# A fused state-space and SwiGLU kernel on one core: the hand-written order of steps rewritten behind step 150, outputs of a pair in two steps, weight powers in two passes, last bank in two halves

## The chip, the core and the metric

One core of a Trainium2 chip. The metric is the time of the kernel on the device in microseconds (us); the kernel before was run three times for its median, and one more execution was recorded by the profiler. TensorE (PE) does the matrix products, VectorE (DVE), ScalarE (ACT) and GpSimd (POOL) the rest, SyncE (SP) issues the transfers.

## The reference

Batch 4, 8 heads, 768 steps, head size 32, 16 states; the result of the first part is read as 3072 tokens of 256 numbers for the second.

```python
for c in range(nc):                       # chunks of 32 steps
    cum = np.cumsum(la, axis=-1)          # la = log a
    L = np.exp(cum[..., :, None] - cum[..., None, :]) * causal
    M = np.einsum('bhin,bhjn->bhij', Cc, Bc) * L
    y_intra = np.einsum('bhij,bhjd->bhid', M, xc)
    y_inter = np.einsum('bhin,bhnd->bhid', Cc, state) * np.exp(cum)[..., None]
    y[:, :, sl] = y_intra + y_inter
    state = decay_full * state + sum_j(B_j x_j decay_from_j)
x = y.transpose(0, 2, 1, 3).reshape(3072, 256)
xn = x / np.sqrt(np.mean(x * x, axis=-1) + 1e-6) * rms_g
out = (silu(xn @ w_gate) * (xn @ w_val)) @ w_out      # 256 -> 1536 -> 256
```

## The kernel before, in words

**Tiles.** The 3072 tokens are 12 *pairs* p of 256 tokens (the state-space part works on them, in halves of 64 tokens from pair 2 on) and 6 *blocks* of 512 tokens (two pairs each; the feed-forward part works on them). The 1536 hidden features are 12 tiles f of 128.

**The state-space part of a pair**, by steps: `x` loads the values (SyncE), `qb`/`qc` load the squares of B and C, `vB`/`vC` turn them, `Tt` and `Td` make the transposed factors T, `spread`, `sub`, `ex`, `ca` make the decays L of a group of heads, `A` multiplies x by the decayed B (TensorE, 28 small products of 32x64), `S` adds that into the running state (VectorE, needs `A`), `y` makes the pair's outputs: first 12 or 16 products of T with the states (recorded as y<-T,S), then 32 products of L with x (y<-L,x). The recorded counts are twice these, since a 4-byte product runs as two passes. The outputs of the two pairs of a block share four banks of PSUM.

**The feed-forward part of a block**, by steps: `sq`, `sqa`, `ms`, `rs`, `rb`, `xn` make the norm. Block 0's features 0 and 1 are multiplied with the outputs before the norm (`early`), which is put on behind. `xH`, `xL`, `xK` split the normed values into three parts, and `X.blk.f.m` (m: 0 gate, 1 value) multiplies them as six products of 128x512. In block 0, features 2 to 7 are multiplied whole instead (`F.blk.f.m`, four passes). Behind `X` or `F` stand `silu` (ScalarE) and `hid` (VectorE, gate times value), then `hH`, `hL`, `hK` split the hidden features, and `OX.blk.f.b` multiplies them with the weights of the way out into bank b of the block's two (block 0: whole, `OF`). Blocks 1 to 4 make their output transposed with 128x512 products (L1197), the last block in 128x256 products (L1203), two groups of 128 tokens in a bank. `put.blk.b` copies a bank of results and issues the transfers out: in blocks 1 to 4 a transpose on VectorE and four transfers, in blocks 0 and 5 a copy (`put` on ScalarE, `putv` on VectorE) and two transfers.

**The weights.** `fetch` loads a strip of weights, `pow` (L272, ScalarE) makes from the high 16 bits of each word the power of two of its exponent, in three passes, `man` (L301) and `wt` (L307) use it on VectorE to form the weight, `wH`, `wL`, `wM` its three parts.

**What sets the order.** No scheduler: one string, `order`, lists 1177 steps, each named with its group (`i:` first steps and weights, `p:` pairs, `b:` blocks), its kind and its numbers. They are emitted in this order, and every engine executes its own instructions in the order in which they were emitted. Buffers come from rings (8 banks of PSUM, and on the on-chip memory 22 and later 29 places of 128x512 and four smaller rings). A place goes back to its ring when its counted uses are through, so the order also decides which buffer an instruction writes to and whom it waits for.

Of the kernel before, what the change touches and what calls it, by code (L numbers as in the profile page):

```python
# [9 lines left out]
FP32 = mybir.dt.float32  # L10
F32R = mybir.dt.float32r
# [39 lines left out]
def kernel(  # L51
# [222 lines left out]
    def power(k):  # L274
        words16, u, shape = fetched[k]
        n = shape[1] * shape[2]
        parts[k, "eb"] = eb = h.take(1, "e")
        e = eb.tile
        g = e.rearrange("p (a b) -> p a b", a=shape[1])
        b16 = e.bitcast(I16)[:, 0:n].rearrange("p (a b) -> p a b", a=shape[1])  # L280
        activation(out=g, in_=words16, func=AF.Relu, scale=1.0 / 16, bias=kinks[:, 0:1])
        activation(out=g, in_=g, func=AF.Prelu, scale=-1.0, bias=kinks[:, 1:2],
                   alpha=2.0 ** -20)
        activation(out=b16, in_=g, func=AF.Prelu, scale=-2.0 ** 27, bias=kinks[:, 2:3],
                   alpha=2.0 ** -20)
        parts[k, "e"] = b16
# [3 lines left out]
    def uses_whole(k):  # L290

        if k < 2:
            return 2
        f = 2 * (k // 2) if k < 12 else 2 * (k - 12)
        return sum((gv_mode(blk, g) == 4) if k < 12 else 2 * ((blk, g) in O4)
                   for g in (f, f + 1) for blk in range(NBLK))
# [70 lines left out]
    kinks = const.tile([P, 3], FP32, name="kinks")  # L367
# [501 lines left out]
    yts, sqs = {}, {}  # L869
# [37 lines left out]
    def outputs(p):  # L907

        n, blk = p % 2, p // 2
        if n == 0:  # L910
            ps["y", blk] = [bank((P, 512), 2, "y") for u in range(4)], set()
        (four, opened), s = ps["y", blk], st[p]

        def product_y(k, u, i, rows, **operands):
            o = four[2 * k + u][1]
            nc.tensor.matmul(out=o[rows, (2 * n + i) * HC:(2 * n + i + 1) * HC],  # L916
                             start=(k, u, rows.start) not in opened, stop=True,
                             skip_group_check=True, **operands)
            opened.add((k, u, rows.start))

        for i in range(2):
            for q in range(NQ):
                for u in range(2):
                    if (2 * p) % NC == 0 and i == 0 and u == 0:
# [3 lines left out]
                    product_y(q // 2, u, i, slice(o, o + 64),  # L928
                              lhsT=S[r].rearrange("p t d -> p (t d)"),
# [3 lines left out]
        opened |= {(k, u, o) for k, u, o_ in opened for o in (o_, o_ + 32)}  # L933
        for i in range(2):
            for hd in range(NH):
                for u in range(2):
                    o = 32 * ((hd + 2 * u) % 4)
                    product_y(hd // 4, u, i, slice(o, o + 32), lhsT=s["x"][halves[u], i, hd],
                              rhs=Ls[p][halves[u], i, hd], tile_position=(HC * u, o))
        s["xb"].used()  # L940
        s["Tb"].used()
# [118 lines left out]
    def modes(blk):  # L1060
        return [gv_mode(blk, f) for f in range(NF)]

    def x_high(blk, t, scaled):
        n = modes(blk).count(3)
        xparts[blk, t, 0] = b = h.take(2 * n + 2, "xh")
# [3 lines left out]
    def x_part(blk, t, i):  # L1069

        xparts[blk, t, i] = b = h.take(2 * modes(blk).count(3), "x" + "hlk"[i])
# [13 lines left out]
    GV4 = {(0, 2), (0, 3), (0, 4), (0, 5), (0, 6), (0, 7)}  # L1085
    O4 = {(0, 0), (0, 1), (0, 2), (0, 3), (0, 4), (0, 5), (0, 6), (0, 7), (0, 8), (0, 9), (0, 10), (0, 11)}

    def gv_mode(blk, f):
        return 0 if blk == 0 and f < 2 else 4 if (blk, f) in GV4 else 3

    def uses_of_x(blk):
        return 6 * (3 in modes(blk)) + 2 * modes(blk).count(4)
# [19 lines left out]
    def normed(f):  # L1112
        banks, gv = ps.pop(("gv", f))
        us[0, f] = h.take(2, "u")
        hx[0, f] = h.take(2, "hx")
# [12 lines left out]
    def hidden(f):  # L1128
        v = view(hx[0, f], [P, TB])
        ub = us.pop((0, f))  # L1130
        nc.vector.tensor_tensor(out=v, in0=view(ub, [P, TB]), in1=v, op=ALU.mult)
# [23 lines left out]
    def silu_gv(blk, f):  # L1155
# [3 lines left out]
                   scale=GAIN if blk == 0 and gv_mode(0, f) == 3 else 1.0)  # L1159
        b.used()  # L1160

    def hide_gv(blk, f):
        v = view(hx[blk, f], [P, TB])
        b, o = gvs.pop((blk, f, 1))
        if (blk, f) in O4 and (blk or gv_mode(blk, f) == 4):
            nc.vector.tensor_tensor(out=v, in0=v, in1=o, op=ALU.mult)
        else:
            nc.vector.scalar_tensor_tensor(out=v, in0=o, scalar=GAIN, in1=v, op0=ALU.mult,  # L1168
                                           op1=ALU.mult)
        b.used()  # L1170

    def hid_high(blk, f, scaled):
        hh[blk, f] = b = h.take(4, "hh")
# [3 lines left out]
    def hid_part(blk, f, i, engine=nc.vector):  # L1177

        (hl, hk)[i - 1][blk, f] = b = h.take(2, "h" + "hlk"[i])
# [9 lines left out]
    OT = {1, 2, 3, 4}  # L1189

# [94 lines left out]
    def token_out():  # L1285
# [46 lines left out]
        "A": additions, "S": states, "y": outputs,  # L1332
# [16 lines left out]
        "OF": o_whole, "OX": o_split,  # L1349
        "put": lambda blk, b: put(blk, b, ac.copy),  # L1350
# [32 lines left out]
        i:wM.10 i:wL.10 b:exps.4 i:wL.6 b:X.0.11.0 p:vB.5 i:fetch.16 b:X.0.8.0 b:hid.0.2 i:wt.14
        b:rb.1 p:spread.11 i:man.15 i:wt.11 i:wM.2 p:dT.4 i:wHv.11 p:spread.10 i:wt.15 i:wH.7
        i:pow.13 p:scale.5 b:OF.0.5.0 p:subp.11 b:OF.0.4.0 i:man.9 b:hid.0.7 p:qc.4 p:vB.4 i:pow.9
        p:vC.5 i:fetch.17 b:X.0.10.0 i:wM.11 i:wH.4 b:OF.0.6.0 i:wt.13 i:wL.11 p:x.5 p:qb.6 b:xn.1.1
        b:OF.0.7.1 b:xn.1.0 i:wt.9 b:silu.0.9 b:OF.0.4.1 b:OF.0.1.1 b:xH.1.1 b:OF.0.7.0 p:sub.8
        b:X.0.11.1 b:xH.1.0 i:wH.9 b:OF.0.6.1 i:wM.3 b:X.0.10.1 b:OF.0.5.1 i:wL.9 b:silu.0.8 i:wM.9
        b:X.0.8.1 b:silu.0.10 b:xK.1.0 b:xL.1.0 p:qb.7 b:silu.0.11 p:ex.11 b:hid.0.11 p:x.4
        b:X.0.9.1 i:pow.16 p:ca.11 b:hid.0.8 p:ex.8 b:xK.1.1 b:xL.1.1 i:wH.12 b:OF.0.2.0 i:man.16  # L1390
        p:vC.4 b:hid.0.3 b:X.1.10.0 b:hid.0.9 i:wH.13 p:Tt.4.1 b:hid.0.10 p:ca.8 p:vB.7 i:pow.17
        b:X.1.1.0 i:man.17 i:wL.7 p:spread.9 b:X.1.11.1 i:wL.3 b:OF.0.3.0 b:X.1.11.0 p:scale.4
        b:silu.1.10 b:silu.1.1 i:wt.17 p:x.6 p:A.4 i:wM.0 i:wt.16 p:S.4 p:Tt.5.1 b:X.1.10.1
        b:OF.0.8.1 p:qb.9 p:A.5 p:sub.9 p:Tt.5.0 p:qc.6 p:subp.10 p:ex.10 b:OF.0.11.0 p:vB.6
        b:hid.1.10 p:ex.9 p:ca.9 b:OF.0.8.0 b:OF.0.10.0 p:ca.10 b:OF.0.9.0 p:dT.5 p:S.5 p:Tt.4.0
        i:wH.17 b:silu.1.11 b:gb.2 i:wL.4 b:X.1.0.0 i:wH.5 i:wL.5 i:wM.7 b:OF.0.2.1 b:L.2.3 i:wL.13
        b:OF.0.11.1 b:L.2.0 b:L.2.1 b:OF.0.10.1 b:silu.1.0 b:hid.1.11 p:Td.4 i:wH.14 b:L.2.2 p:vC.6
        p:qc.9 p:Td.5 p:scale.6 b:X.1.9.0 p:qc.7 b:hH.1.10 p:y.4 b:put.0.0 p:y.5 b:X.1.0.1 p:vB.9
        b:sq.2.0 p:x.7 i:wH.15 b:silu.1.9 b:X.1.1.1 p:spread.12 b:sq.2.1 i:wM.5 b:OF.0.3.1 p:vC.7
        b:yt.2.0 p:scale.9 i:wM.12 b:X.1.6.0 i:wM.4 p:A.6 b:yt.2.1 b:hK.1.10 p:dT.6 b:silu.1.6  # L1400
        b:sqav.2 b:X.1.5.1 i:wM.17 i:wH.16 p:spread.13 p:subp.12 b:hid.1.1 i:wL.17 b:X.1.5.0 b:ms.2
        p:spread.14 b:OF.0.9.1 p:ex.12 p:S.6 b:X.1.9.1 b:table.4 i:wM.13 b:put.0.1 b:silu.1.5
        p:scale.7 i:wL.16 p:Tt.7.1 b:rs.2 i:wM.16 i:wL.12 b:hH.1.1 b:X.1.2.0 i:exps b:hid.1.0
        b:X.1.3.0 p:spread.15 b:rb.2 p:vC.9 p:Tt.6.1 p:qb.10 b:hH.1.11 b:hid.1.9 b:hid.1.5 b:hH.1.0
        b:X.1.4.1 p:A.7 p:sub.14 b:silu.1.2 b:X.1.8.1 p:sub.13 b:hK.1.0 p:qb.8 p:S.7 b:X.1.8.0
        p:Tt.7.0 b:silu.1.8 b:X.1.4.0 b:hLp.1.1 p:ex.14 b:hid.1.8 b:hL.1.10 p:sub.15 b:X.1.6.1
# [113 lines left out]
```

## Time and profile before

| | |
|---|---|
| median of 3 runs | 369.09 us (368.76 to 369.15) |
| the profiled execution | 368.75 us, of which the span from first to last instruction is 367.0 us |
| mean granted TensorE clock | 0.998 |
| busy: TensorE, VectorE, ScalarE, GpSimd | 360.1, 276.7, 203.1, 75.0 us |
| recorded instructions: TensorE, VectorE, ScalarE | 3293, 514, 346 |
| feature products, three-part, L1150 | 768 in three groups of 83.0, 79.4 and 79.1 us |
| moved by transfers | 27.95 MB |

Busy times are sums over the whole span. Products are pipelined, so a recorded length (400 ns for a 128x512 product) is longer than the distance between the starts of two of them; where it matters, starts are compared. In the chain of waits, "issue" is time in which an engine waited for nothing that the profile shows, "SPq" is SyncE's queue at work on an instruction.

### The profile page before, as it was taken

Reading aid. Unit: us, or ns where it says so; the run is one execution under the profiler, and the core shown is the slowest. Engines: PE = TensorE matmul, PEld = TensorE weight load, DVE = VectorE, ACT = ScalarE, POOL = GpSimd, SP = SyncE. Lnnn points to the kernel's source line nnn. Section 1 sums busy time; section 2 is a strip of 40 time slices with the busy share of each in tenths; the row PEclk is TensorE's granted clock in tenths of the full one; section 3 lists DMA queues with packets and bytes.
Section 4 is the critical chain, followed back from the end, with each engine's and each line's share of the span. In section 5 each row is a group of like instructions: output and inputs, shape, how many; then the busy total and the mean of one; then the engine's idle time right before and its main releaser. Section 6 shows DMA issues by size and latency. Waiting matters only on the chain.

```text
span 367.0 us, 8226 instructions
## 1 busy us (share of the span) xinstructions
PE 360.1 (98%) x3293; PEld 280.8 (77%) x3293; DVE 276.7 (75%) x514; ACT 203.1 (55%) x346; POOL 75.0 (20%) x79
## 2 busy tenths in 40 slices
PE   8999989999999999999999999999999999999995
PEld 5677455887887777787877778877888888888895
DVE  6899897998998699875867896656447595346790
ACT  3899959999658864486237577034630222421310
POOL 4032010022301311352102316100303001131350
PEclk9999999999999999999999999999999999999999
DMA  7979872564564323542114210110000002001011
GB/s 104 207 136 275 220 292 43 170 143 105 91 120 104 107 47 78 121 63 63 33 30 121 63 29 2 30 30 2 7 29 2 0 10 50 0 0 29 2 30 57
DMA packets 94702, 27.95 MB, mean 76 GB/s; under 512 B 77544, under 2 KB 92616, under 8 KB 94664
## 3 DMA queue, kind: packets, MB, share of 16 engines
q1 hardware_dynamic: 92584, 27.30, 32.6%
q8 instruction: 26, 0.43, 0.5%
q10 hardware_dynamic: 2080, 0.13, 0.4%
q14 instruction: 12, 0.10, 0.1%
HBM read 23.68 MB, written 3.74 MB: 75 GB/s over the span
## 4 chain that ended last, share of the span: by engine, by line
PE 87%; SPq 3%; DVE 3%; ACT 2%; DMA 2%; issue 2%; POOL 0%; ACTq 0%; POOLq 0%; DVEq 0%
PE gv L1150 44%; PE o L1197 18%; PE o L1203 7%; PE gv L1140 4%; PE y L916 3%; PE gv L1105 2%; SPq L186 2%; PE g L766 2%; PE A L831 1%; DMA bq<-in_B_dram 1%; PE g L759 1%; DMA wr<-in_moe_w_out_dram 1%; ACT e L272 1%; SPq L654 1%; PE y L892 1%
## 5 line engine op out<-in xcount | busy, mean ns | idle before, releaser
L272 ACT ACTIVATE hx<-gv 128x512 f32<-128x512 f32 x70 | 40.4, 597 | 90.4 <-PE gv L1150 46.5
L1150 PE MATMUL gv<-xh,wh 128*128 128x512 f32 x256 | 83.0, 405 | 0.0
L1150 PE MATMUL gv<-xl,wp 128*128 128x512 f32 x256 | 79.4, 391 | 0.0
L1150 PE MATMUL gv<-xk,wp 128*128 128x512 f32 x256 | 79.1, 390 | 0.0
L1078 POOL TENSOR_TENSOR hl<-hx,hh 128x512 fp32r<-128x512 f32 x27 | 40.2, 1499 | 150.4 <-PE o L1197 99.5
L1168 DVE SCALAR_TENSOR_TENSOR hx<-gv,hx 128x512 f32<-128x512 f32 x64 | 43.0, 683 | 27.1 <-PE gv L1150 20.6
L1080 DVE SCALAR_TENSOR_TENSOR hk<-hx,hh 128x512 fp32r<-128x512 f32 x60 | 47.5, 810 | 18.6 <-PE o L1197 14.4
L1150 PEld LDWEIGHTS gv<-xl,wp 128*128 128x128 f32 x256 | 48.0, 188 | 10.8 <-DVE xl L1078 0.4
L1150 PEld LDWEIGHTS gv<-xk,wp 128*128 128x128 f32 x256 | 48.0, 188 | 10.4 <-DVE xk L1080 0.2
L1150 PEld LDWEIGHTS gv<-xh,wh 128*128 128x128 f32 x256 | 46.6, 188 | 11.0 <-issue 1.1
L1197 PE MATMUL o<-hh,wh 128*128 128x512 f32 x96 | 37.9, 395 | 0.0
L1197 PE MATMUL o<-hl,wp 128*128 128x512 f32 x96 | 37.4, 389 | 0.0
L1197 PE MATMUL o<-hk,wp 128*128 128x512 f32 x96 | 37.3, 389 | 0.0
L329 ACT ACTIVATE hh<-hx 128x512 fp32r<-128x512 f32 x35 | 21.6, 626 | 25.3 <-PE o L1197 15.8
L1078 DVE TENSOR_TENSOR hl<-hx,hh 128x512 fp32r<-128x512 f32 x33 | 24.1, 729 | 9.9 <-PE o L1197 7.6
L272 ACT ACTIVATE e<-e,kinks 128x512 f32<-128x512 f32 (+1 forms) x36 | 26.0, 722 | 1.2
L323 DVE SCALAR_TENSOR_TENSOR wp<-wh,w 128x512 fp32r<-128x512 f32 x36 | 24.6, 702 | 0.6 <-ACT wh L329 0.5
L632 POOL TENSOR_SCALAR_AFFINE_SELECT L<-L 64x512 f32<-64x512 f32 (+1 forms) x22 | 17.1, 776 | 34.1 <-ACT L L272 32.3
L1203 PE MATMUL o<-w,hx 128*128 128x256 f32 x96 | 23.5, 385 | 0.0
L1140 PE MATMUL gv<-xn,w 128*128 128x512 f32 x48 | 22.4, 603 | 0.0
L266 ACT ACT_TABLE_LOAD x17 | 21.8, 1283 | 1.1 <-PEq L1504 0.8
L1197 PEld LDWEIGHTS o<-hh,wh 128*128 128x128 f32 x96 | 18.0, 188 | 4.1 <-issue 0.2
(173 smaller groups left out, 525.4 us busy)
## 6 DMA issues: line engine op xcount, KB each, us to landing
L<-rowd SPq DMA_DIRECT2D x32, 128.0 KB
x<-in_x_dram SPq DMA_DIRECT2D x24, 128.0 KB
wr<-in_moe_w_out_dram SPq DMA_DIRECT2D x6, 511.5 KB
wr<-in_moe_w_gate_dram SPq DMA_DIRECT2D x5, 511.5 KB
wr<-in_moe_w_val_dram SPq DMA_DIRECT2D x5, 511.5 KB
out_dram<-ob SPq DMA_DIRECT2D x32, 64.0 KB
bc<-in_B_dram SPq DMA_DIRECT2D x23, 64.0 KB
bc<-in_C_dram SPq DMA_DIRECT2D x23, 64.0 KB
```

Source lines behind the costliest of these rows:

```text
L266: nc.scalar.preload_act_table_set("natural_log_exp_and_others")
L272: nc.scalar.activation(**operands)
L323: nc.vector.scalar_tensor_tensor(out=(low_parts, mixed_parts)[i][k], in0=high_parts[k], scalar=(-UP, GAIN)[i], in1=view(ws[k], shape), op0 ...
L329: nc.scalar.activation(out=out, in_=in_, func=AF.Copy, scale=scale)
L632: nc.gpsimd.affine_select(out=L[r], in_=L[r], pattern=[[0, L.shape[1]], [1, HC]], compare_op=ALU.is_ge, fill=0.0, base=0, channel_multipli ...
L1078: engine.tensor_tensor(out=out, in0=v, in1=high, op=ALU.subtract)
L1080: nc.vector.scalar_tensor_tensor(out=out, in0=v, scalar=REST, in1=high, op0=ALU.mult, op1=ALU.subtract)
L1140: nc.tensor.matmul(out=o, lhsT=view(ws[k], fetched[k][2])[:, t, f % 2 * P:][:, 0:P], rhs=xn[:, t], start=(t == 0), stop=(t == 1))
L1150: nc.tensor.matmul(out=o, lhsT=weights_of(m, t, f)[part], rhs=view(x, [P, TB], F32R), start=(part == t == 0), stop=(part == 2 and t == 1))
L1168: nc.vector.scalar_tensor_tensor(out=v, in0=o, scalar=GAIN, in1=v, op0=ALU.mult, op1=ALU.mult)
L1197: nc.tensor.matmul(out=o, lhsT=w[:, b * P:(b + 1) * P], rhs=v, start=opens, stop=True, skip_group_check=True)
L1203: nc.tensor.matmul(out=o[:, j * DM:(j + 1) * DM], lhsT=v[:, tk], rhs=w, start=opens, stop=True, skip_group_check=True)
```

## The change

The first 150 steps of `order` stay as they are. All steps behind them stand in another order, and there are 1200 steps in all. Four pieces of code change with it:

- `y` becomes two steps, `yi` (the products with the states) and `ya` (those with x), so that other steps can stand between them.
- `power` makes its result in two passes on ScalarE. The constants in `kinks` are two.
- For the second bank of the last block, the 12 steps `OX.5.f.1` (six products each) and `put.5.1` (a 128x512 copy on ScalarE, two transfers) are replaced by 24 steps `OY.f.j` (three products each), which fill one bank for each 128 tokens j, and by `puta.1` (ScalarE) and `putva.0` (VectorE), each a copy of 128x256 and one transfer.
- Whether a feature of block 0 uses whole weights can be chosen for gate and value apart; the set that is chosen is the same as before. `hide_gv` always uses the form of the product that also scales.

```diff
-        activation(out=g, in_=words16, func=AF.Relu, scale=1.0 / 16, bias=kinks[:, 0:1])
-        activation(out=g, in_=g, func=AF.Prelu, scale=-1.0, bias=kinks[:, 1:2],
+        activation(out=g, in_=words16, func=AF.Prelu, scale=-1.0 / 16, bias=kinks[:, 0:1],
                    alpha=2.0 ** -20)
-        activation(out=b16, in_=g, func=AF.Prelu, scale=-2.0 ** 27, bias=kinks[:, 2:3],
+        activation(out=b16, in_=g, func=AF.Prelu, scale=-2.0 ** 27, bias=kinks[:, 1:2],
                    alpha=2.0 ** -20)
...
-        for k, v in enumerate((1152.0, 256.0, -1792.0 * 128.0)):
+        for k, v in enumerate((-896.0, -1792.0 * 128.0)):
...
-    def outputs(p):
...
+    def outputs_of_states(p):
+        s = st[p]
         for i in range(2):
             for q in range(NQ):
                 for u in range(2):
...
+                    product_y(p, q // 2, u, i, o, 64, lhsT=S[r].rearrange("p t d -> p (t d)"),
                               rhs=s["T"][r, i, 3, halves[u]], tile_position=(32 * q, o))
...
+    def outputs_of_chunks(p):
+        s, blk = st[p], p // 2
         for i in range(2):
             for hd in range(NH):
                 for u in range(2):
...
+                    product_y(p, hd // 4, u, i, o, 32, lhsT=s["x"][halves[u], i, hd],
                               rhs=Ls[p][halves[u], i, hd], tile_position=(HC * u, o))
...
+    def product_apart(f, j):
+        if j not in apart:
+            apart[j] = bank((P, DM), NF + 1, "o")
+        place, o = apart[j]
+        tk = slice((2 + j) * P, (3 + j) * P)
+        for k, w in enumerate(out_weights_of(f)):
+            v = (hh, hl, hk)[k][NBLK - 1, f]
+            nc.tensor.matmul(out=o, lhsT=view(v, [P, TB], F32R)[:, tk], rhs=w,
+                             start=place.uses == NF + 1 and k == 0, stop=True,
+                             skip_group_check=True)
+            v.used()
+        place.used()
+
+    def put_apart(j, copy):
+        ob = h.take(1, "ob")
+        out_sb = view(ob, [P, DM])
+        place, o = apart[j]
+        copy(out=out_sb, in_=o)
+        rows = slice(T - (2 - j) * P, T - (1 - j) * P)
+        nc.sync.dma_start(out=out[rows], in_=out_sb)
...
-        b:OX.5.0.0 b:putv.5.0 b:OX.5.2.1 b:OX.5.1.1 b:put.5.1
+        b:OY.4.1 b:OY.2.1 b:OY.1.1 b:putv.5.0 b:OY.1.0 b:puta.1 b:putva.0
```

**TensorE around pairs 2 and 3.** Before, in program order (gv are feature products, here whole ones of block 0; A the additions of pair 2 and then 3; the rows with y the outputs of pair 2 and then 3; counts are instructions in the program):

```order
L1140 MATMUL gv<-xn,w 128x512 x8
L831 MATMUL A<-x,Bd 32x64 x12
L1140 MATMUL gv<-xn,w 128x512 x2
L831 MATMUL A<-x,Bd 32x64 x16
L1140 MATMUL gv<-xn,w 128x512 x2
L916 MATMUL y<-T,S 64x64 x16
L916 MATMUL y<-L,x 32x64 x32
L1140 MATMUL gv<-xn,w 128x512 x2
L916 MATMUL y<-T,S 64x64 x12
L916 MATMUL y<-L,x 32x64 x32
```

Now, on the same engine at the same place:

```order
L1149 MATMUL gv<-xn,w 128x512 x6
L830 MATMUL A<-x,Bd 32x64 x28
L1149 MATMUL gv<-xn,w 128x512 x6
L916 MATMUL y<-T,S 64x64 x16
L916 MATMUL y<-L,x 32x64 x32
L916 MATMUL y<-T,S 64x64 x12
L916 MATMUL y<-L,x 32x64 x32
L1149 MATMUL gv<-xn,w 128x512 x4
```

The additions of the two pairs now stand side by side, three feature steps stand between them and the outputs (one before), and the outputs of the two pairs stand side by side.

**SyncE around the values of pair 5.** Before (bc<-in_C with bc<-in_B in the row above it is a `qc` step, bq<-in_B a `qb` step; the first x row is pair 5, the second pair 4, the third pair 6):

```order
L173 DMA bc<-in_B_dram 128x8x16 x2
L186 DMA bc<-in_C_dram 128x1x128 x2
L238 DMA wr<-in_moe_w_out_dram 128x2x1023
L205 DMA x<-in_x_dram 128x8x32 x2
L186 DMA bq<-in_B_dram 128x1x128 x4
L205 DMA x<-in_x_dram 128x8x32 x2
L654 DMA L<-rowd 64x512 x2
L205 DMA x<-in_x_dram 128x8x32 x2
```

Now (the first x row is pair 4, the second pair 6, the third pair 5; the two qc steps are those of pairs 6 and 7):

```order
L205 DMA x<-in_x_dram 128x8x32 x2
L653 DMA L<-rowd 64x512 x2
L173 DMA bc<-in_B_dram 128x8x16 x2
L186 DMA bc<-in_C_dram 128x1x128 x2
L205 DMA x<-in_x_dram 128x8x32 x2
L173 DMA bc<-in_B_dram 128x8x16 x2
L186 DMA bc<-in_C_dram 128x1x128 x2
L205 DMA x<-in_x_dram 128x8x32 x2
```

The values of pair 5 were the first of the three to be issued and are now the last, behind the squares of pairs 6 and 7.

**SyncE at the end of the program.** Before, the transfers out of block 4 (32x16x32) and of block 5:

```order
L1229 DMA out_dram<-ob 32x16x32 x16
L1236 DMA out_dram<-ob 128x256 x4
```

Now:

```order
L1260 DMA out_dram<-ob 32x16x32 x16
L1267 DMA out_dram<-ob 128x256 x2
L1218 DMA out_dram<-ob 128x256 x2
```

The last four transfers are the same in number and size; the last two now belong to two copies.

More of the change, by code (lines that the diff above doesn't have):

```diff
@@ L905, in first_outputs, with outputs_of, product_y @@
         s["Tb"].used()
-    def outputs(p):
[L909 to L919, printed above, removed]
+    def outputs_of(p):
+        if p // 2 not in yparts:
+            yparts[p // 2] = [bank((P, 512), 2, "y") for u in range(4)], set()
+            ps["y", p // 2] = yparts[p // 2]
+        return yparts[p // 2]
+    def product_y(p, k, u, i, first, n, **operands):
+        four, opened = outputs_of(p)
+        groups = {(k, u, r) for r in range(first, first + n, 32)}
+        o = four[2 * k + u][1]
+        nc.tensor.matmul(out=o[first:first + n, (p % 2 * 2 + i) * HC:(p % 2 * 2 + i + 1) * HC],
+                         start=not groups & opened, stop=True, skip_group_check=True, **operands)
+        opened |= groups
+    def outputs_of_states(p):
+        s = st[p]
         for i in range(2):
```

277 lines of the change are left out of this document (140 added, 137 removed).

## The prediction

> **What bounds the kernel now.** I read the page's busy times first, then the chain of waits, then who waited for whom, then single stretches.
>
> ```profile
> PE 360.1 (98%) x3293; PEld 280.8 (77%) x3293; DVE 276.7 (75%) x514; ACT 203.1 (55%) x346; POOL 75.0 (20%) x79
> PE 87%; SPq 3%; DVE 3%; ACT 2%; DMA 2%; issue 2%; POOL 0%; ACTq 0%; POOLq 0%; DVEq 0%
> PE y L916 <- issue: 1.3, 2, 1.0
> ```
>
> TensorE is busy for 360.1 of 367.0 us, it is 87% of the chain, and the list of its waits (third line) has nothing above 1.3 us. The change keeps every product: the last block's second bank gets the same 128x256 products in another arrangement, and the set of features with whole weights is the same. So TensorE's work cannot shrink by arithmetic. What can shrink is the time around it: waits, the passage from big to small products and back, and the tail. What can grow is waiting for the other engines. A busy TensorE hides short gaps, so I read its starts:
>
> ```profile
> 138.03 0.39 PE L1197 MATMUL o<-hl,wp 128*128 128x512 f32 x1
> 138.26 0.39 PE L1197 MATMUL o<-hk,wp 128*128 128x512 f32 x1
> 138.58 0.46 PE L916 MATMUL y<-T,S 32*64 32x64 f32 x24
> 138.97 0.86 PE L916 MATMUL y<-L,x 64*32 64x64 f32 x64
> 139.76 0.50 PE L1197 MATMUL o<-hh,wh 128*128 128x512 f32 x1
> 140.09 0.40 PE L1197 MATMUL o<-hl,wp 128*128 128x512 f32 x1
> 140.33 0.39 PE L1197 MATMUL o<-hk,wp 128*128 128x512 f32 x1
> 141.06 0.31 PE L916 MATMUL y<-L,x 64*32 64x64 f32 x6
> 141.72 0.80 PE L916 MATMUL y<-L,x 64*32 64x64 f32 x58 [0.35 <-issue]
> ```
>
> Starts of a big product are 0.23 us apart (138.03, 138.26). The step into the small ones takes 0.32 us (138.26 to 138.58), the first big one behind them 0.33 us (139.76 to 140.09).
>
> **Term A: fewer passages between big and small products.** Going in costs 0.32 - 0.23 = 0.09 us, the first big one 0.10 us. The group of 64 ends at 138.97 + 0.86 = 139.83; a small product is recorded as 0.22 us long (row below), so its last one started at 139.61, and 0.15 us pass until 139.76. One island of small products thus costs 0.09 + 0.15 + 0.10 = 0.34 us beside its work. Two kinds of small product side by side cost one such 0.15 us: the 24 end at 139.04, the last of them started at 138.81, the next kind starts at 138.97.
>
> ```profile
> L916 PE MATMUL y<-L,x 64*32 64x64 f32 x640 | 9.1, 224 | 1.3 <-issue 1.3
> ```
>
> From the first step behind the products of the raw y (early) to the end, the steps of before make 29 islands with 11 joints inside them (10 of them the two halves of a pair's outputs); those of after make 20 islands with 20 joints, since A.2 stands beside A.3, y of pair 2 beside pair 3, A.5 beside A.4, A.7 beside A.6 and ms.2. That is 9 x 0.34 - 9 x 0.15 = 1.7 us less. Three of the pairs' outputs are now split by big products (pairs 6, 8, 10); they are counted in the 20. If joints cost nothing the term is 3.1 us, if they cost as much as an island it is nearly 0; the rows above say 0.15, so I take -1.7. [...]
>
> **Term B: two waits inside small products.**
>
> ```profile
> 44.69 0.39 PE A L831 x32
> 45.08 1.91 PE gv L1140 x4
> 46.99 1.10 PE y L916 x78
> 48.09 0.99 issue
> 49.09 0.33 PE y L916 x11
> ...
> 138.65 1.18 PE y L916 x76
> 139.83 0.89 PE o L1197 x3
> 140.72 0.66 PE y L916 x38
> 141.37 0.35 issue
> 141.72 0.80 PE y L916 x51
> ```
>
> In y.2 TensorE stands until 49.09, though its last product started at 48.09 - 0.22 = 47.87: 1.2 us. In y.7 it stands from 141.06 + 0.31 - 0.22 = 141.15 to 141.72: 0.57 us. The profile names no releaser ("issue"). I read them as the instruction stream running dry:
>
> ```profile
> q8 instruction: 26, 0.43, 0.5%
> ```
>
> 26 packets of 0.43 MB are 16.5 KB each, and 2 x 3293 products and weight loads over 26 are 253 instructions a packet, so a block of 256. I counted blocks through TensorE's order (a 4-byte product is two passes, so four instructions). The block before the first wait starts in A.3 (44.69) and the next falls at the end of y.2; the block before the second starts in y.6 (138.65) and ends in the middle of y.7. Resumption comes 49.09 - 44.69 = 4.4 us and 141.72 - 138.65 = 3.1 us after those starts: the next block needs that long, and the dense stretches ran through theirs in 3.2 and 2.5 us. In the new order the first of these blocks holds the rest of A.3, three whole products of 1.72 us each (1.91 less the island's ends) and y.2: about 6.5 us, over 4.4. The second holds three products of block 1's outputs (0.68 us each) where there was one: 2.5 + 1.36 less the part of y that left it gives about 3.4 us, over 3.1. The corresponding blocks of pairs 8 and 9 and of 10 and 11 come to about 3.5 us. So both waits go: -1.8 us; the bounds are 0 (they come back elsewhere) and -1.8.
>
> [...]
>
> **Term C: the tail.**
>
> ```profile
> 362.51 2.14 SPq L1236 DMA_DIRECT2D out_dram<-ob  x4
> 362.84 0.28 PE L1203 MATMUL o<-wp,hk 128*128 128x256 f32 x1
> 363.23 0.59 ACT L1233 COPY ob<-o 128x512 f32<-128x512 f32 x1 [12.97 <-PE o L1203]
> L735 DVE TENSOR_TENSOR T<-tp,dT 128x256 f32<-128x256 f32 x2 | 0.9, 431 | 0.1
> ```
>
> Today the last product ends at 363.12, ScalarE copies 128x512 in 0.59 us, and SyncE issues two transfers behind it, until 362.51 + 2.14 = 364.65. Now the last bank holds half: VectorE copies 128x256, for which I take 0.43 us (last row, another VectorE operation of this size out of PSUM), and one transfer follows, about 0.4 us less of issue. Saved: 0.16 + 0.38 = 0.5 us. The two put.4 steps now stand late on VectorE and bring eight transfers onto SyncE shortly before (about 0.5 us each, 4 us); if they are not through, the saving is 0, so the bounds are 0 and -0.8 (a shorter copy).
>
> **Term D: what VectorE, ScalarE and SyncE now do to TensorE.** The powers of two passes take one 0.72 us pass each off ScalarE:
>
> ```profile
> L272 ACT ACTIVATE e<-e,kinks 128x512 f32<-128x512 f32 (+1 forms) x36 | 26.0, 722 | 1.2
> 30.00:90.00 60.00, 58.92 (x533) 38.75 (x532) 54.85 (x108) 54.66 (x90) 9.12 (x9) 1.00 0.63 173
> DVE w L307 <- ACT e L272: 2.8, 3, 2.2
> DVE A L848 <- PE A L831: 1.0, 1, 1.0
> DVE T L193 <- DMA bq<-in_B_dram: 1.0, 1, 1.0
> ```
>
> 18 x 0.72 = 13 us less on ScalarE, which is not TensorE's bound, so by itself 0. It matters through VectorE. In 30 to 90 us VectorE is busy 54.85 of 60 us and waits 4.8 us (three last lines), 2.8 of them for powers. The new order wants more of it earlier: the steps behind the common 150 up to S.4 are 119 VectorE instructions instead of 112, and X.1.9.1 waits for S.4. Before, those 112 ran from 32.2 us until
>
> ```profile
> 91.50 0.59 DVE L860 SCALAR_TENSOR_TENSOR S<-S,fcol,A 128x64 f32<-128x64 f32 x2
> 92.39 0.36 PE A L831 x24
> ```
>
> 92.1, that is 59.9 us, of which 55.1 not waiting: 0.49 us each. So 119 take 58.5 us and end at 90.7 without any wait, at 95.5 with the old 4.8 us. TensorE gets there, by its steps' order, 1.5 us of products behind where A.5 stood (92.39), less 1.2 us of term B and 0.75 of term A: about 91.9. The wait is between 0 and 3.6 us. The 2.8 us for powers should go (two passes, and pow.7 no longer behind the squares of y), the 1.0 us for A.3 too (three big products now stand between A.3 and y.2), and new small ones come: about 2 us of waiting, S.4 at 92.7, wait 0.8. Other places I put at 0.2 in sum, so +1.0, with bounds 0 and +5 (the SyncE rival below).
>
> **Sum.** The profiled execution took 368.75 us (span 367.0). -1.7 - 1.8 - 0.5 + 1.0 = -3.0 gives 365.75. It lies 0.34 us below the median of the runs shown, 369.09, so the median should come to 366.0.
>
> **Rivals.**
>
> *SyncE holds x.5 back, and it becomes slower.* The transfers of x for pair 5 now stand behind qc.6, x.6 and qc.7 on SyncE's queue, and qc.7 waits until wL.4 has freed its buffer (about 82.6 us, 46.3 us of VectorE work behind 32.3 and 4 of waits and slow instructions). Prices of this queue in this stage:
>
> ```profile
> 78.46 2.90 SPq L186
> ...
> 82.58 4.20 DMA bq<-in_B_dram
> ```
>
> An issue can take 2.9 us and a transfer 4.2 us to land. With usual issues of 0.6 us: four for qc.7, two for x.5, and 2 to 4.2 us to land give 88 to 90.4; TensorE wants A.5 at about 88.5 to 89. With one slow issue in each of the two steps x.5 lands at 82.6 + 4.7 + 3.5 + 4.2 = 95.0, TensorE waits some 6.3 us, S.4 and S.5 go with it, and the sum is -4.0 + 6.3 = +2.3: 371.4 us. Against it: before, x.4 was issued until 84.5 and used at 89.35 without trouble. It decides from x.5 landing behind about 93.5. Chance 0.16.
>
> *The waits of term B are not the instruction stream.* Then they stay or move, term B is 0, and term A may be only half: -0.9 - 0.5 + 0.0 = -1.4, so 367.7 us. For it: no row ties a fetch to a wait. Against it: both waits stand where the count puts a block's end. Chance 0.14. [...]
>
> *The gains are just eaten*, term D being +4: no change, 369.1. Chance 0.06. That the steps don't come out as said is excluded by the order of the instructions.
>
> **How the numbers follow.** The forecast has 0.64. Its own range: everything favourable (A -2.5, B -1.8, C -0.8, D 0) is 369.1 - 5.1 = 364.0; D at +2.5 is 367.5. The second rival lies at 367.7, no change at 369.1; to hold 8 in 10 the range has to reach just beyond that, to 369.5, and leaves out SyncE's case. I set 363.8 to 369.5. A difference below 0.2% (0.7 us) can't be told from none in this kernel. Faster by more: forecast and second rival, 0.78; within: 0.06; slower: 0.16.
>
> **What would show it.** Right: no "issue" wait inside y.2 and y.7; A.2 and A.3 as one group of 56; a last copy of 128x256 and one issue behind it; fewer than 2 us in all of TensorE's waits between 80 and 110 us. Wrong: a wait of TensorE at A.5 behind x, at X.1.9.1 behind S.4, or new "issue" waits in the small products of pairs 8 to 11; then the term named is the failed one.

## The result and the profile after

The changed kernel takes 371.4 us (median of 6 runs, 370.34 to 373.15); the kernel before, on the same chip, 368.96 us (6 runs). The ratio is 1.0069 with a 95% interval of 1.0046 to 1.0093: slower by 0.5 to 0.9%, where 366.0 was forecast. The profiled execution took 373.15 us with a span of 371.4, the longest of the six; the other spans are 368.6 to 369.7.

The page of the changed kernel, its busy times, TensorE's granted clock in 40 slices (tenths, 9 is 90% or more) and the chain of waits:

```profile
PE 361.1 (97%) x3293; PEld 283.8 (76%) x3293; DVE 277.6 (75%) x514; ACT 189.9 (51%) x328; POOL 78.2 (21%) x79
PEclk9999987999999999999999999999999999999999
PE 83%; DVE 7%; DMA 3%; ACT 2%; issue 2%; POOL 1%; SPq 1%; DVEq 0%; ACTq 0%
```

ScalarE lost its 13 us (203.1 to 189.9) and TensorE has the same 3293 products. New is the dip of the clock in the sixth and seventh slice. What TensorE waited for:

```profile
PE gv L1149 <- ACT hx L272: 3.4, 1, 3.4
PE gv L1159 <- DVE L L788: 0.5, 1, 0.5
```

The line "y <- issue" of before is gone. In its place TensorE waits once for 3.4 us. Where, shows TensorE's timeline (start, length, operation):

```profile
42.97 0.79 PE L830 MATMUL A<-x,Bd 64*32 64x64 f32 x56
43.69 5.42 PE L1149 MATMUL gv<-xn,w 128*128 128x512 f32 x12
49.04 0.49 PE L916 MATMUL y<-T,S 32*64 32x64 f32 x32
49.46 0.86 PE L916 MATMUL y<-L,x 64*32 64x64 f32 x64
50.24 0.46 PE L916 MATMUL y<-T,S 32*64 32x64 f32 x24
50.63 0.86 PE L916 MATMUL y<-L,x 64*32 64x64 f32 x64
54.86 6.54 PE L1149 MATMUL gv<-xn,w 128*128 128x512 f32 x8 [3.37 <-ACT hx L272]
61.23 3.62 PE L1234 MATMUL o<-w,hx 128*128 128x256 f32 x16
```

A.2 and A.3 are one group of 56 and the outputs of pairs 2 and 3 run without a stop, as forecast. Then F.0.2.1 and F.0.3.1 wait for a silu, and when they run, their eight products take 6.37 us to the next group, 2.8 us more than the same two steps where nothing was waited for (51.51 to 55.05 in the kernel with the strips first, told of below). The stretches around it say why (busy time of each engine, and behind them the granted clock and the DMA engines' share):

```profile
50.00:52.00 2.00, 1.49 (x118) 1.17 (x106) 0.00 (x0) 0.00 (x0) 0.00 (x0) 1.00 0.89 272
52.00:54.00 2.00, 0.00 (x0) 0.00 (x0) 1.27 (x3) 1.17 (x2) 0.00 (x0) 0.94 1.09 361
54.00:56.00 2.00, 1.14 (x2) 0.63 (x3) 2.00 (x5) 1.97 (x5) 0.00 (x0) 0.50 1.00 380
...
60.00:62.00 2.00, 2.00 (x7) 1.22 (x6) 2.00 (x4) 1.98 (x5) 0.06 (x1) 0.85 0.12 27
```

From 50 to 52 us VectorE and ScalarE do nothing, while the DMA engines are full (0.89 to 1.09), and from 53.8 us, 1.1 us before the wait ends, until 60.6 us TensorE is granted half its clock (0.50). ScalarE's timeline, VectorE's waits and, below them, SyncE's timeline:

```profile
47.20 0.72 ACT L272 ACTIVATE e<-e,kinks 128x512 int16<-128x512 f32 x1
52.79 0.77 ACT L272 ACTIVATE e<-wr,kinks 128x512 f32<-128x512 int16 x1 [4.88 <-DMA wr<-in_moe_w_val_dram]
54.23 1.06 ACT L272 ACTIVATE hx<-gv 128x512 f32<-128x512 f32 x2
```

```profile
DVE w L300 <- DMA wr<-in_moe_w_val_dram: 4.5, 1, 4.5
DVE T L193 <- DMA bc<-in_C_dram: 1.8, 1, 1.8
```

```profile
39.72 1.03 SPq L173 DMA_DIRECT2D bc<-in_B_dram  x2
40.80 2.50 SPq L186 DMA_DIRECT2D bc<-in_C_dram  x2
43.40 1.11 SPq L186 DMA_DIRECT2D bq<-in_B_dram  x2
45.07 0.51 SPq L241 DMA_DIRECT2D wr<-in_moe_w_val_dram  x1
```

ScalarE stands for 4.88 us at pow.7 until weight strip 7 has landed; the two silus (54.23) that free TensorE's banks are queued behind it. VectorE stands for 4.5 us at man.7, which reads the same strip, and some 10 us later for 1.8 us at vC.5, the turn of the squares of C of pair 5. The strip is issued at 45.07, behind the squares of pair 4 (qc.4, 39.72 and 40.80) and qb.5. In the list of steps fetch.7 went from place 156 to 173, qc.4 from 290 to 158, and pow.7 from 228 to 215. The same strip in the kernel before:

```profile
37.23 2.60 SPq L241 DMA_DIRECT2D wr<-in_moe_w_val_dram  x1
```

The tail, SyncE and the last copy:

```profile
361.53 5.50 SPq L1260 DMA_DIRECT2D out_dram<-ob  x8
367.12 0.92 SPq L1267 DMA_DIRECT2D out_dram<-ob  x2
368.14 0.91 SPq L1218 DMA_DIRECT2D out_dram<-ob  x2
366.34 0.42 DVE L1216 COPY ob<-o 128x256 f32<-128x256 f32 x1 [1.40 <-PE o L1206]
```

The last copy ends at 366.76, but SyncE is busy with the eight transfers of the two put.4 steps until 367.03 and issues the last one until 369.05.

**Where the 4.4 us of span went** (in this execution, which is 1.75 us over the median). The sums over many starts are added up from the two traces. More: 3.4 the wait at F.0.2.1, 2.8 the half clock behind it, 0.5 a wait at 106.8 us, 1.2 the tail (from the last product's start to the end of the span 5.4 us, before 4.2), 0.6 the first 26 us, where executions differ anyway (the same product of the norm starts at 25.76 before, 26.38 after, 26.84 in the kernel of before with the two-pass powers, whose order is the same), 0.6 inside the groups of small products, whose starts are further apart now (6.8 us above the usual distance in sum, before 6.2). Less: 1.8 the two waits inside y, 1.7 going into small products, coming out of them and passing between their kinds (7.6 us in sum, before 9.3), 1.1 the first big product behind them (2.2 us, before 3.3).

That makes +9.1 - 4.6 = +4.5, so 0.1 us is left over. The rest of the question was which of the causes is the root: the power that stands too early, the strip that comes too late, or VectorE.

### The profile page after: what moved, and what is told of

Read it like the earlier page. It is cut to its first block, busy times and chain, and to the rows that moved or that the text cites. A ratio compares the mean times of both kernels' runs of the same rounds, so it can differ in the third digit from the quotient of the medians.

```text
span 371.4 us, 8201 instructions
## 1 busy us (share of the span) xinstructions
PE 361.1 (97%) x3293; PEld 283.8 (76%) x3293; DVE 277.6 (75%) x514; ACT 189.9 (51%) x328; POOL 78.2 (21%) x79
## 4 chain that ended last, share of the span: by engine, by line
PE 83%; DVE 7%; DMA 3%; ACT 2%; issue 2%; POOL 1%; SPq 1%; DVEq 0%; ACTq 0%
PE gv L1159 42%; PE o L1228 16%; PE o L1234 5%; PE gv L1149 5%; PE y L916 2%; PE o L1206 2%; DMA wr<-in_moe_w_val_dram 2%; PE gv L1112 2%; DVE wp L322 1%; POOL L L631 1%; PE g L758 1%; PE A L830 1%; PE g L765 1%; DVE L L788 1%; PE e L595 1%
## 5 line engine op out<-in xcount | busy, mean ns | idle before, releaser
L1159 PE MATMUL gv<-xh,wh 128*128 128x512 f32 x256 | 81.3, 399 | 0.5 <-DVE L L788 0.5
L1174 DVE SCALAR_TENSOR_TENSOR hx<-gv,hx 128x512 f32<-128x512 f32 x70 | 47.0, 682 | 27.5 <-PE gv L1159 18.7
L1082 DVE SCALAR_TENSOR_TENSOR hk<-hx,hh 128x512 fp32r<-128x512 f32 x60 | 50.0, 845 | 20.8 <-PE o L1228 20.3
L631 POOL TENSOR_SCALAR_AFFINE_SELECT L<-L 64x512 f32<-64x512 f32 (+1 forms) x22 | 22.1, 1005 | 37.2 <-ACT L L272 36.3
L1149 PE MATMUL gv<-xn,w 128*128 128x512 f32 x48 | 24.8, 665 | 3.4 <-ACT hx L272 3.4
L1234 PE MATMUL o<-w,hx 128*128 128x256 f32 x96 | 22.6, 382 | 0.0
L1228 PEld LDWEIGHTS o<-hk,wp 128*128 128x128 f32 x96 | 18.0, 188 | 3.8
```

The costliest lines, as they stand in the source:

```text
L631: nc.gpsimd.affine_select(out=L[r], in_=L[r], pattern=[[0, L.shape[1]], [1, HC]], compare_op=ALU.is_ge, fill=0.0, base=0, channel_multipli ...
L1082: nc.vector.scalar_tensor_tensor(out=out, in0=v, scalar=REST, in1=high, op0=ALU.mult, op1=ALU.subtract)
L1149: nc.tensor.matmul(out=o, lhsT=view(ws[k], fetched[k][2])[:, t, f % 2 * P:][:, 0:P], rhs=xn[:, t], start=(t == 0), stop=(t == 1))
L1159: nc.tensor.matmul(out=o, lhsT=weights_of(m, t, f)[part], rhs=view(x, [P, TB], F32R), start=(part == t == 0), stop=(part == 2 and t == 1))
L1174: nc.vector.scalar_tensor_tensor(out=v, in0=o, scalar=gain(blk, f), in1=v, op0=ALU.mult, op1=ALU.mult)
L1228: nc.tensor.matmul(out=o, lhsT=w[:, b * P:(b + 1) * P], rhs=v, start=opens, stop=True, skip_group_check=True)
```

## The experiments

**First: move the power out of the way, in two ways, and move the transfer.** The first kernel:

```diff
-b:F.0.4.1 i:pow.7 i:man.7 b:silu.0.5 i:hid.0 b:silu.0.3 i:wt.8
+b:F.0.4.1 b:silu.0.5 i:hid.0 b:silu.0.3 i:pow.7 i:man.7 i:wt.8
```

> The changed kernel, with pow.7 and man.7 moved behind silu.0.3; nothing else moves, all transfers stand as they were. Theory 1 (ScalarE stands at pow.7 until strip 7 lands, and the silus queued behind it hold the two banks that TensorE needs): TensorE's wait of 3.4 us at the whole products of block 0 goes, and the half clock behind it too, which cost 2.9 us in the profiled run; that run was 1.75 us over the median, so the median falls by about 4.5 us, from 371.4 to 366.9. Theory 2 (the late strip itself is the bound: its weight is needed soon behind): the wait only moves to the next user of strip 7, and the time stays within 1 us of 371.4.

Measured (e1_pow7_late): 371.07 us, ratio 1.0071 (1.005 to 1.0093). Nothing gained, so theory 1 in this form fell. Its profiled execution had a granted clock of 0.95 throughout, so its waits are not compared. The other five had mean clocks of 0.997 to 1.000 and took 370.5 to 372.7 us, so the time stays also where the half clock does not come. The next kernel suggests what happened:

```diff
-i:pow.7 i:man.7 b:silu.0.5 i:hid.0 b:silu.0.3
+b:silu.0.5 i:pow.7 i:man.7 i:hid.0 b:silu.0.3
```

> The changed kernel, with pow.7 and man.7 moved between silu.0.5 and silu.0.3, so that one of the two banks comes free in time and 1.7 us of whole products cover that much of the wait. Theory 1: TensorE's wait at the whole products shrinks from 3.4 to 1.6 us. If the half clock follows only a long wait, it stays away, and the median is about 368.5; if any wait over a microsecond brings it, the products behind it are still slowed by about 2.9 us and the median is about 370.

Measured (e4_pow7_between): 371.44 us, ratio 1.007 (1.0053 to 1.0088). What TensorE waited for:

```profile
PE gv L1149 <- ACT yt L992: 1.8, 1, 1.8
PE gv L1149 <- DVE hx L1174: 0.9, 1, 0.9
PE gv L1149 <- ACT hx L272: 0.7, 1, 0.7
```

The wait at F.0.2.1 shrank from 3.4 to 0.7, the half clock stayed away, and the time came back a little later: F.0.6.1 waits 1.8 us for the copies of y (yt), which stand on ScalarE behind the powers of strips 14, 10 and 15, and F.0.7.1 waits 0.9 us for VectorE, which had stood for 1.83 us at vC.5 until 62.95. Now the transfer:

```diff
-i:man.5 p:qc.4 p:qb.5 i:norm.1
+i:man.5 p:qb.5 i:norm.1
...
-i:fetch.14 b:silu.0.2 i:man.3 i:fetch.7 i:wt.4
+i:fetch.14 b:silu.0.2 i:man.3 i:fetch.7 p:qc.4 i:wt.4
```

> The changed kernel, with the transfers of qc.4 moved behind those of strip 7 on SyncE's queue; ScalarE's order stays. Theory 1: strip 7 is issued about 3.7 us earlier (1.03 + 2.50 us of issue are no longer ahead of it) and lands 3 to 5 us earlier, so ScalarE stands at pow.7 for under 2 us and TensorE's wait is under 0.5 us: 367 us. Theory 2 (the transfers share the DMA engines, so order on the queue hardly matters): strip 7 lands less than 1.5 us earlier, TensorE still waits about 2 us, and the time is 369 to 371.

Measured (e2_qc4_late): 371.87 us, ratio 1.0101 (1.0078 to 1.0124). ScalarE's timeline:

```profile
51.38 0.72 ACT L272 ACTIVATE e<-e,kinks 128x512 int16<-128x512 f32 x1
56.15 0.79 ACT L272 ACTIVATE e<-wr,kinks 128x512 f32<-128x512 int16 x1 [4.05 <-DMA wr<-in_moe_w_gate_dram]
```

pow.7 no longer waits: strip 7 is issued at 41.53 instead of 45.07. But ScalarE comes to pow.10 sooner and stands there for 4.05 us, for strip 10, which is issued at 49.79 (49.11 in the changed kernel). TensorE's waits sum to 3.9 us. Theory 1 is right on strip 7 and wrong on the time: one strip earlier leaves the next one late.

**Second: the two-pass powers alone, in the order of before.**

```diff
-        activation(out=g, in_=words16, func=AF.Relu, scale=1.0 / 16, bias=kinks[:, 0:1])
-        activation(out=g, in_=g, func=AF.Prelu, scale=-1.0, bias=kinks[:, 1:2],
+        activation(out=g, in_=words16, func=AF.Prelu, scale=-1.0 / 16, bias=kinks[:, 0:1],
                    alpha=2.0 ** -20)
```

> The kernel before with the two-pass powers alone, order unchanged. Theory 1 (ScalarE is not the bound there): 13 us less of ScalarE and no more than 0.3 us off the time, 368.7. Theory 2 (VectorE's 2.8 us of waits for powers reach TensorE): 1 us or more off, below 368.0.

Measured (e3_two_pass): 368.71 against 368.82 us, ratio 0.9998 (0.9985 to 1.0012). ScalarE's passes are not worth time by themselves.

**Third: all the powers, or all the strips.** First the powers behind the squares:

```diff
-b:F.0.4.1 i:pow.7 i:man.7 b:silu.0.5
-p:yi.3 i:pow.14 i:wt.12 i:pow.10 i:fetch.11 b:hid.0.5 i:wt.7 i:wHv.8 i:man.10 p:ya.3 b:sq.1.0
-i:wL.8 b:F.0.2.1 b:F.0.3.1 b:hid.0.4 i:pow.15
+b:F.0.4.1 b:silu.0.5
+p:yi.3 i:wt.12 i:fetch.11 b:hid.0.5 i:wHv.8 p:ya.3 b:sq.1.0 b:sq.1.1 b:yt.1.1 b:yt.1.0
+i:wL.8 b:F.0.2.1 b:F.0.3.1 b:hid.0.4 i:pow.7 i:man.7 i:pow.14 i:pow.10 i:wt.7 i:man.10 i:pow.15
```

> The changed kernel, with the squares and copies of block 1 (sq.1.0, sq.1.1, yt.1.1, yt.1.0) put right behind ya.3 on ScalarE and the powers of strips 7, 14, 10 and 15 (with man.7, man.10 and wt.7) behind them; transfers unchanged. Theory A (ScalarE meets powers of strips that have not landed ahead of the steps that free TensorE's banks, wherever these stand): TensorE's waits between 50 and 66 us fall from 3.7 to 5 us to under 1, and the median comes to about 368. Theory B (the late strips themselves bound: their weights are needed soon behind): the wait moves to VectorE's weights and the time stays at 370 or more.

Measured (e5_squares_first): 372.21 us, ratio 1.0105 (1.0074 to 1.0137). Theory B had the time, theory A only the place: the waits at the whole products are gone, and one of the same size stands at the first split products. VectorE, which makes the parts, had waited 2.1 us for a power and 2.0 us at vC.5:

```profile
PE gv L1159 <- DVE xl L1080: 4.0, 1, 4.0
```

Then the strips ahead of the squares of pairs 4 and 5:

```diff
-i:man.5 p:qc.4 p:qb.5 i:norm.1
+i:man.5 i:norm.1
...
-b:table.2 p:qb.4 i:pow.8
+b:table.2 i:pow.8
...
-i:pow.10 i:fetch.11 b:hid.0.5
+i:pow.10 i:fetch.11 p:qb.5 p:qc.4 p:qb.4 b:hid.0.5
```

> The changed kernel, with the transfers of qb.5, qc.4 and qb.4 moved behind the strip of fetch.11 on SyncE's queue, so that six strips are issued 4.6 to 6.4 us earlier; ScalarE's order unchanged. Theory A, and with it the reading that the squares' transfers among the strips are the root: pow.7 and pow.10 wait under 0.5 us each, TensorE's waits between 50 and 66 us sum to under 0.7 us, the median is 367.5 to 368. Theory C (the transfers share their engines, which are full from 44 to 58 us, so order does little): pow.10 or pow.15 still waits over 2 us and the time is 370 or more.

Measured (e6_strips_first): 371.92 us, ratio 1.0083 (1.0059 to 1.0107). The powers no longer wait (from 40 to 64 us ScalarE has no gap above 0.05 us ahead of one), and still TensorE stands for 3.3 us, later:

```profile
64.02 3.62 PE L1149 MATMUL gv<-xn,w 128*128 128x512 f32 x4 [3.28 <-DVE hx L1174]
```

VectorE's timeline of this kernel names a second stop. In the changed kernel it lasted 1.8 us and TensorE did not wait for it; here, where the engines come there sooner, it lasts 3.9:

```profile
58.17 0.42 DVE L331 TENSOR_SCALAR wh<-w 128x512 fp32r<-128x512 f32 x1
62.48 0.64 DVE L193 STREAM_TRANSPOSE T<-bc 128x256 f32<-128x256 f32 x1 [3.88 <-DMA bc<-in_C_dram]
```

That is vC.5, which turns the squares of C of pair 5. It went from place 293 to 259, while its transfer, qc.5, stayed (241 and 240); it now stands ahead of hid.0.3 and of the split of x.

**Fourth: the second stop alone, and both stops.** The edit is the same in three kernels:

```diff
-b:F.0.6.1 p:vC.5 b:ms.1
+b:F.0.6.1 b:ms.1
...
-b:xK.0.0 b:xL.0.0 p:spread.11
+b:xK.0.0 b:xL.0.0 p:vC.5 p:spread.11
```

> The changed kernel with vC.5 alone moved behind xL.0.0; strips and powers stand as in it. Theory D: pow.7 still holds ScalarE until strip 7 lands, TensorE waits some 3 us at the whole products of block 0, and the median stays at 370.5 to 371.5. Theory E: the same. If vC.5 were the whole cause, it would fall to about 367.

Measured (e11_vC5_late): 371.88 us, ratio 1.0079 (1.005 to 1.0108): nothing by itself, and TensorE still waits 2.3 us for the silu at F.0.2.1. With the strips first:

> As e6_strips_first, and vC.5 moved behind xL.0.0 on VectorE. Theory D (two engines stand in turn at the head of their own queues: ScalarE at pow.7 until a late strip lands, VectorE at vC.5 until the late squares of pair 5 land; with one relieved the other one shows): with both out of the way TensorE's wait of 3.3 us goes, and the half clock behind it (1.7 us), so the median falls from 371.9 to about 366.9. Theory E (VectorE has too much work in this stage, and the wait at vC.5 only stands where it would be late anyway): TensorE still waits about 3 us there or at the split values behind, and the median stays above 370.

Measured (e10_strips_vC5): 367.12 us, ratio 0.9944 (0.9928 to 0.9961). Theory D holds, theory E falls: 4.8 us went (5.1 by the ratios, which set each kernel against the one before on its own chip), and the kernel is faster than the one before. TensorE's longest waits, one in the warm-up at the start aside:

```profile
PE gv L1159 <- DVE hx L1174: 0.5, 1, 0.5
PE gv L1159 <- DVE L L788: 0.4, 1, 0.4
```

With the powers behind the squares instead:

> As e5_squares_first (all transfers as in the changed kernel, only ScalarE's powers behind its squares), and vC.5 moved behind xL.0.0. Theory D: the wait of 4.0 us for the split values goes and the half clock behind it, so the median falls from 372.2 to about 367, without a transfer being moved. Theory E: it stays above 370.

Measured (e13_squares_vC5): 369.37 us, ratio 1.002 (1.0002 to 1.0037), between the two theories. 2.8 us went, not 5. VectorE now waits 3.7 us for a power, and TensorE 1.4 us for the split values:

```profile
DVE w L306 <- ACT e L272: 3.7, 1, 3.7
PE gv L1159 <- DVE xl L1080: 1.4, 1, 1.4
```

No power waits for a strip here. VectorE begins on strip 7 at 52.26, but ScalarE makes pow.7 only at 54.86, behind the squares and copies, so it is the place of the power that holds VectorE up. That the late strips are the root of the first stop is shown by the kernels with the strips first, in which the powers stand where they stood and ScalarE has no gap above 0.05 us ahead of one from 40 to 64 us, with or without vC.5 moved; moving the powers instead shifts a part of the stop to VectorE.

**Fifth: the tail.** The first attempt moved the two put.4 steps forward:

```diff
-b:OX.4.2.1 b:OY.3.1
+b:OX.4.2.1 b:put.4.1 b:put.4.0 b:OY.3.1
...
-b:OX.5.11.0 b:put.4.1 b:OY.6.1 b:put.4.0 b:OX.5.7.0
+b:OX.5.11.0 b:OY.6.1 b:OX.5.7.0
```

> As e6_strips_first, and put.4.1 and put.4.0 moved forward behind OX.4.2.1. If the tail's 1.2 us come from the eight transfers that these two issue so late, SyncE is free when the last copy ends, the time from TensorE's last product to the end of the span falls from 5.4 to about 4, and the median is 1.2 us below that of e6_strips_first. If VectorE, which then makes two transposes (1.3 us) ahead of the hidden parts of features 6 and 7, holds TensorE up, at most half of that is left.

Measured (e7_strips_put): 373.52 us (median of five; the sixth, the profiled one, took 905.48), ratio 1.0138 (1.0107 to 1.0168), 1.6 us worse than without the move. The only trace is that of the execution of 905.48 us, so that VectorE's 1.3 us of transposes held TensorE up is argued, not shown. The second attempt moved them less far and relieved VectorE:

```diff
-b:hL.5.10 b:hHv.5.6 b:OY.8.1
+b:hL.5.10 b:hH.5.6 b:OY.8.1
...
-b:hK.5.6 b:hHv.5.4 b:hL.5.7 b:hLp.5.2 b:hK.5.10 b:OY.7.0
+b:hK.5.6 b:hH.5.4 b:hL.5.7 b:hLp.5.2 b:hK.5.10 b:put.4.1 b:put.4.0 b:OY.7.0
...
-b:OY.6.0 b:hHv.5.1 b:hK.5.1
+b:OY.6.0 b:hH.5.1 b:hK.5.1
...
-b:OX.5.11.0 b:put.4.1 b:OY.6.1 b:put.4.0 b:OX.5.7.0
+b:OX.5.11.0 b:OY.6.1 b:OX.5.7.0
```

> As e10_strips_vC5, and at the end: the first parts of hidden features 6, 4 and 1 of the last block made by ScalarE, which is idle there, and put.4.1 and put.4.0 moved forward behind hK.5.10. The eight transfers then start about 3 us earlier, SyncE is free when the last copies end, and the time from TensorE's last product to the end of the span falls from 5.4 to about 4.2: 1.2 us below e10_strips_vC5. If the transposes make VectorE late, TensorE waits in the last 15 us and less than half of it is left.

Measured (e12_strips_vC5_tail): 366.04 us, ratio 0.9912 (0.9894 to 0.9929), 1.08 us below the kernel without it, and the fastest of all:

```profile
348.72 4.11 SPq L1260 DMA_DIRECT2D out_dram<-ob  x8
358.85 0.82 SPq L1267 DMA_DIRECT2D out_dram<-ob  x2
360.33 0.81 SPq L1218 DMA_DIRECT2D out_dram<-ob  x2
```

The eight transfers are through at 352.83, 6 us before the next ones are issued, and from the last product's start (359.97) to the end of the span (363.53) pass 3.6 us, where the kernel without these edits has 4.9. VectorE's relief and the earlier transfers were not tried apart.

**Sixth: the waits inside y.** In the kernel before, one big step was moved out of each gap between two outputs:

```diff
-p:y.2 i:hid.0 b:F.0.4.1 p:y.3
+b:F.0.4.1 p:y.2 i:hid.0 p:y.3
...
-p:y.6 i:wL.14 b:hid.1.7 b:hHv.1.9 b:xL.2.0 b:OX.1.1.1 p:y.7
+b:OX.1.1.1 p:y.6 i:wL.14 b:hid.1.7 b:hHv.1.9 b:xL.2.0 p:y.7
```

> The kernel before, with F.0.4.1 moved ahead of y.2 and OX.1.1.1 ahead of y.6. If the two waits inside y are the instruction stream, the block before the first holds 1.7 us more of products and the first wait goes, and the block before the second holds 0.7 us less, so the second grows by about 0.7 us, from 0.6 or 0.8 to 1.3 or 1.5 us. With two islands fewer (0.19 us each) the time falls by about 0.5 us, to 368.3. If the waits have another cause, the first stays at 0.5 to 1.2 us or the second at 0.6 to 0.8 us.

Measured (e9_move_F): 367.54 against 368.69 us, ratio 0.9975 (0.996 to 0.999). The time fell by more than the 0.5 us expected. The first wait went, the second stayed and did not grow:

```profile
48.63 0.49 PE L916 MATMUL y<-T,S 32*64 32x64 f32 x32
49.05 0.86 PE L916 MATMUL y<-L,x 64*32 64x64 f32 x64
49.84 0.46 PE L916 MATMUL y<-T,S 32*64 32x64 f32 x24
...
137.52 0.46 PE L916 MATMUL y<-T,S 32*64 32x64 f32 x24
137.91 0.97 PE L916 MATMUL y<-L,x 64*32 64x64 f32 x64
...
139.23 0.31 PE L916 MATMUL y<-L,x 64*32 64x64 f32 x6
139.98 0.80 PE L916 MATMUL y<-L,x 64*32 64x64 f32 x58 [0.45 <-issue]
```

139.98 - (139.23 + 0.31 - 0.22) = 0.66 us, where 1.3 to 1.5 were expected; by the words of the expectation the second wait speaks for another cause. The packets of the instruction queue, whose starts the trace has, explain it better than my count from a block's first instruction. They start at 46.71 and 139.32 in the kernel before, whose waits end at 49.09 and 141.72; at 47.23 and 138.83 in the same order with the two-pass powers (ends 49.47 and 141.54); at 137.64 here (end 139.98). Five waits end 2.2 to 2.7 us behind the start of a packet. With the big step moved, the packet also starts earlier, 0.1 us behind the first product of y.6 instead of 0.7. That an instruction fetch ends these waits is supported by the five coincidences, not shown by a kernel that moves the fetch alone; what starts it is open.

## Why the prediction was wrong

**Term A, fewer islands: right in sign, its size partly luck.** Summed over all starts behind 25 us, going in, coming out, the first big product behind and the joints, the four things that the term was made of, take 12.5 us before and 9.8 now: -2.8. The islands were counted rightly, the joints not: of the 20 now, 16 are a change of kind, at 0.12 us each (11 before, at 0.14), and additions side by side show no such step. Against this, +0.6 us came inside the groups, 0.5 of it in the additions, whose starts in the second half of a group of 56 are up to 17 ns apart instead of 7; no term had it. So -2.2 in all, where -1.7 was worked out.

**Term B, the two waits inside y: right here.** Both went, -1.8. Moving one big step ahead of y.2 took the first wait away, which speaks against the rival that they are something else, but does not exclude it. The clock of the step was wrong (4.4 and 3.1 us from a block's entry), which the second wait of the sixth experiment showed. The block of 256 was an estimate from 253 instructions a packet; no run shows where a block begins. If the fetch is what ends these waits, 0.5 to 1.2 us of it stood open in these dense small products.

**Term C, the tail: wrong sign.** The copy did shrink (0.42 us), but I let "not through" cost only the saving. The eight transfers took 5.50 us at 361.53 where I had put 4 us, and the tail became 1.2 us longer instead of 0.5 shorter.

**Term D is the step that failed.** It was +1.0 us, with +5 as its upper bound, and came to 6.7 in the profiled execution (3.4 the wait, 2.8 the half clock, 0.5 at 106.8 us). I priced ScalarE's part as a saving: 13 us less, "by itself 0", and counted it as a gain that pow.7 no longer stands behind the squares of y. In the profile of before, ScalarE's 3.8 us wait at those squares was harmless, because the powers behind them found their strips landed:

```profile
52.39 1.21 ACT L272 ACTIVATE sq<-y 128x256 f32<-128x256 f32 x4 [3.77 <-PE y L916]
54.67 0.77 ACT L272 ACTIVATE e<-wr,kinks 128x512 f32<-128x512 int16 x1
```

In front of them, pow.7 waits for a transfer, and what is queued behind it are the steps that free TensorE's banks. I had gone through SyncE's queue for x.5 only, and not asked of each power and each turn that moved forward when its own transfer is issued now. The second stop, vC.5, is the same omission on VectorE. I looked for the narrow place at 84 to 95 us and put 0.8 us there; no wait for S.4 or x.5 came, and the loss was at 51 to 66 us.

**The rival with the right number.** "SyncE holds x.5 back" gave 371.4 us, the measured median, but not by its mechanism:

```profile
90.37 1.04 SPq L205 DMA_DIRECT2D x<-in_x_dram  x2
```

x.5 was issued until 91.41 and A.5 ran at 95.00 without waiting for it. Nor does the lost time hide such a wait: in the kernel with both stops mended A.5 stands at 89.58, and none of TensorE's waits of 0.2 us or more is for x. SyncE's queue was part of the cause, with another transfer, 45 us earlier.

**The half clock** was in no term. In the profiled execution it cost nearly as much (2.8 us) as the wait that it came with (3.4 us). That it makes the time scatter (370.34 to 373.15 for this kernel) is not shown: the first experiment's kernel scatters from 370.5 to 372.7 at mean clocks of 0.997 to 1.000.

With both stops and the tail mended, the new order measures 366.04, about what the sum said (366.0; its own terms, 365.75 + 0.34, give 366.1). The agreement is chance: A came out 0.5 us larger than its term, and the new tail has an edit that the prediction did not know.

## What to carry to other kernels

When an instruction is moved forward on an engine that runs its instructions in program order, as ScalarE did here (the two silus stood behind pow.7 through its wait of 4.88 us), look up its slowest input, a transfer above all, in the new order, and list what is queued behind it; an engine with time to spare (here ScalarE, busy for 51% of the span) can stop the one that has none (TensorE, 97%, stopped for 3.4 us). When a wait is removed and the time stays, look for a second engine that stands in the same stretch: here two stops hid each other. The fixes of the first alone left 371.1 to 372.2 us, that of the second alone 371.9, and both together 367.1, which is 4.3 us below the changed kernel. Ask of every late group of transfers what will be queued behind it at the end.

## What the runs showed of the hardware

A wait of TensorE can have a second price. Behind waits of up to 1.8 us (pow.7 between the silus) the granted clock stayed at 1.00 (in each stretch of 2 us from 50 to 62 us; 0.997 over the execution); with one of 2.3 us (vC.5 alone moved) it fell to half (0.50). The half clock lasted 3.4 us there, and also with the waits of 3.3 us (strips first: means of 0.56 and 0.59 from 64 to 66 and 66 to 68 us) and 4.0 us (powers behind the squares: 0.59 and 0.56 from 70 to 72 and 72 to 74 us), where the length is worked out from these means at a level of 0.50; with the changed kernel's 3.4 us it lasted 6.8. So it came in one length or twice that, and did not grow with the wait; what decides between the two no run shows. The stretches of the kernel with vC.5 alone moved, clock third from the end:

```profile
52.00:54.00 2.00, 0.43 (x1) 0.44 (x2) 2.00 (x5) 1.97 (x5) 0.00 (x0) 0.85 1.07 402
54.00:56.00 2.00, 2.00 (x3) 0.74 (x3) 2.00 (x6) 1.97 (x3) 0.00 (x0) 0.50 1.03 391
56.00:58.00 2.00, 2.00 (x5) 0.88 (x4) 2.00 (x5) 1.50 (x5) 0.00 (x0) 0.80 0.89 187
```

In these rows the half clock begins at 53.4 us (0.85), 2.1 us behind the start of the wait and 0.2 us before its end. Worked out in the same way, it began 2.3 us behind the start of the wait in the changed kernel, 3.5 us with the strips first and 5.0 us with the powers behind the squares, so these four executions give no one length of idle time that brings it.
